# One exp and eight masked copies for eight exps, and the first half of K multiplied in one go, in a decode attention kernel

## Chip, cores, metric

One core of a Trainium2 chip. The metric is the device time of one execution in microseconds (us). All runs quoted are undisturbed ("fast"). The spans in the profiles are 1.7 to 1.9 us shorter than the device times.

## The reference

Attention with one query per head, softmax over all 4096 positions, no mask:

```python
B, H, Sq, Skv, Dh = 8, 32, 1, 4096, 128        # all bf16, normal * 0.05
scores = jnp.einsum('bhqd,bhkd->bhqk', q, k) * Dh ** -0.5
return jnp.einsum('bhqk,bhkd->bhqd', softmax(scores), v)
```

K and V are 268.4 MB each, and each byte is used once.

## The kernel before

The 256 heads go through in 32 tiles of 8 heads. A tile of K or V is 128 partitions x 256 positions x 128 values: 16 partitions per head. K and V tiles take turns in a ring of three buffers. Engines: DVE multiplies K by q in place and folds the products by halves; PE sums what is left over d by multiplying with the identity; DVE reduces these sums to scores and takes the maximum; ACT makes the weights; PE multiplies weights and V.

Three places matter. The multiply of a quarter (UC = MC = 64 positions):

```python
def product(t, lo, hi):
    for c0 in range(lo, hi, MC):
        part = kt[:, c0 : c0 + MC, :]
        nc.vector.tensor_tensor(out=part, in0=part, in1=qb[:].to_broadcast([P, MC, D]), op=ALU.mult)
        nc.vector.tensor_tensor(out=part[:, :, 0 : D // 2], in0=..., in1=..., op=ALU.add)
        ...                          # in quarters 2 and 3 of most tiles a second fold, to D // 4
```

The weights, which must be zero for the 7 heads that do not own a partition:

```python
nc.vector.tensor_scalar(out=bias[:], in0=own[:], scalar1=nmax[:, 0:1], scalar2=None, op0=ALU.add)
for g in range(G):                   # own holds 0 or -1e30 per head: exp gives 0 for a foreign one
    nc.scalar.activation(out=w[:, :, g, :], in_=sc_g, func=ACT.Exp, bias=bias[:, g : g + 1],
                         scale=scale, accum_out=esum[:, t % R, g : g + 1])
```

And the order within a tile, which is fixed by hand for PE, DVE, ACT and the load queue:

```python
product(t, 0, Q);          sum_over_d(t, 0)
...                        # PE: normalisation, result of t-2, q of t+2
product(t, Q, 2 * Q);      sum_over_d(t, 1);  scores_of(t, 0)
product(t, 2 * Q, 3 * Q);  sum_over_d(t, 2);  scores_of(t, 1)
product(t, 3 * Q, C);      sum_over_d(t, 3);  scores_of(t, 2)
if loop:                   # tiles 1 to 29
    values_loop(t - 1)     # 64 matmuls on PE, weights x V of the tile before
    load("k", t + 1); load("v", t)
scores_of(t, 3); weights_of(t)
```

The load of a V tile goes into the buffer of the K tile just used, that of a K tile into the buffer of the V tile that the value loop has just read.

## Time and profile before

| | before |
|---|---|
| time, median of 3 runs | 1252.86 us (1252.73 to 1252.98) |
| load queue, share of 16 DMA engines | 99.4%, mean 430 GB/s |
| DVE / PE / ACT busy | 83% / 62% / 14% |
| one K and V pair | 38.7 us |

### The profile page before, as it was taken

What the parts mean: (1) busy time and instruction counts of PE and PEld (TensorE: products, weight loads), DVE (VectorE), ACT (ScalarE), POOL (GpSimd) and SP (SyncE); (2) the same over time, 40 slices, a digit from 0 to 9 for tenths busy, and PEclk for the clock granted to TensorE, in tenths of its full rate; (3) what the DMA queues carried; (4) which work ended last, traced back from release to release, by engine and by line L of the source; (5) the groups of instructions that cost most, each with busy time, mean ns of one, the idle gap of its engine ahead of it and who ended that gap; (6) DMA issues with size and microseconds to landing.
All of it is one profiled execution on the core that took longest, in us unless ns stands there. A gap on an engine that the chain in (4) does not pass through costs nothing. (4 is left out here: it accounts for less than half of the span.)

```text
span 1250.9 us, 11080 instructions
## 1 busy us (share of the span) xinstructions
PE 770.4 (62%) x3078; PEld 289.4 (23%) x3078; DVE 1036.1 (83%) x586; ACT 170.7 (14%) x625; POOL 3.5 (0%) x19
## 2 busy tenths in 40 slices
PE   3465567755577555775557755577655776557756
PEld 1122122211222212222122221122221222122222
DVE  7887988888978889887798888988889887898783
ACT  0111011111011110111101111011110111101111
POOL 0000000000000000000000000000000000000000
PEclk9977788777887778877778777788777887778867
DMA  9999999999999999999999999999999999999997
GB/s 404 436 436 435 436 436 432 434 436 434 434 424 430 434 434 436 425 434 434 436 436 434 434 434 430 436 428 434 434 430 424 432 437 436 428 428 428 430 445 324
DMA packets 11577, 537.33 MB, mean 430 GB/s; under 512 B 1824, under 2 KB 2080, under 8 KB 2336
## 3 DMA queue, kind: packets, MB, share of 16 engines
q1 hardware_dynamic: 11216, 536.94, 99.4%
q8 instruction: 14, 0.23, 0.1%
q10 hardware_dynamic: 336, 0.07, 0.0%
q14 instruction: 11, 0.09, 0.0%
HBM read 536.94 MB, written 0.07 MB: 429 GB/s over the span
## 5 line engine op out<-in xcount | busy, mean ns | idle before, releaser
L185 DVE TENSOR_TENSOR kt<-kt,qb 128x8192 bf16<-128x8192 bf16 x128 | 565.3, 4416 | 127.9 <-DMA kt<-in_k_dram 103.5
L205 PE MATMUL ps<-kt,ident 128*128 128x512 bf16 x800 | 265.3, 483 | 432.4 <-DVE kt L193 366.8
L289 PE MATMUL av<-vt,w 128*32 x1740 | 426.1, 399 | 3.8
L188 DVE TENSOR_TENSOR kt<-kt 128x4096 bf16<-128x4096 bf16 x128 | 293.4, 2292 | 4.4
L289 PEld LDWEIGHTS av<-vt,w 128*32 x1740 | 174.4, 100 | 261.2 <-issue 114.4
L205 PEld LDWEIGHTS <-ident 128*128 128x128 bf16 x800 | 87.2, 113 | 597.0 <-issue 550.7
L249 ACT ACTIVATE w<-sc,bias 128x256 bf16<-128x256 f32 x256 | 126.3, 494 | 671.6 <-DVE bias L240 671.6
L217 DVE TENSOR_REDUCE sc<-ps 128x64 f32<-128x512 f32 x128 | 87.8, 686 | 57.3 <-PE ps L205 57.3
L193 DVE TENSOR_TENSOR kt<-kt 128x2048 bf16<-128x2048 bf16 x56 | 68.6, 1225 | 1.9
L345 ACT ACTIVATE comb<-av 32x512 bf16<-32x512 f32 (+1 forms) x32 | 18.8, 586 | 321.6 <-PEq L279 313.5
L275 PE MATMUL av<-vt,w 128*32 128x512 bf16 x116 | 47.1, 498 | 14.6 <-issue 13.4
L249 ACT ACTIVATION_READ_ACCUMULATOR w<-sc,bias 128x1 f32 x256 | 47.7, 187 | 0.0
L275 PEld LDWEIGHTS av<-vt,w 128*32 128x32 bf16 x116 | 6.9, 100 | 55.2 <-issue 55.2
L168 ACT ACTIVATE qg<-qh 8x128 bf16<-8x128 f32 x32 | 8.5, 267 | 73.8 <-PE qh L164 73.8
L317 PE MATMUL av<-vt,w 128*32 128x512 bf16 x190 | 14.7, 411 | 1.6 <-DMA vt<-in_v_dram 1.6
L361 PE MATMUL op<-comb,pick 32*16 32x128 bf16 (+1 forms) x128 | 12.3, 215 | 5.1 <-ACT comb L345 5.0
L229 DVE TENSOR_REDUCE pmax<-sc 128x1 f32<-128x256 f32 x32 | 13.4, 420 | 1.1
L170 PE MATMUL qp<-qg,heads 8*128 8x128 bf16 x32 | 6.9, 216 | 11.4 <-ACT qg L168 11.4
L164 PE MATMUL qh<-q_all,ident 128*8 128x128 bf16 x32 | 7.1, 223 | 8.7 <-DMA q_all<-in_q_dram 8.4
L172 ACT ACTIVATE qb<-qp 128x128 bf16<-128x128 f32 x32 | 8.9, 278 | 9.7 <-PE qp L170 9.7
L361 PEld LDWEIGHTS <-pick 32*16 32x16 bf16 (+1 forms) x128 | 6.8, 84 | 12.4 <-issue 12.0
L317 PEld LDWEIGHTS <-w 128*32 128x32 bf16 x190 | 6.5, 103 | 9.9 <-issue 5.5
(29 smaller groups left out, 47.4 us busy)
## 6 DMA issues: line engine op xcount, KB each, us to landing
kt<-in_k_dram SPq DMA_DIRECT2D x6, 4096.0 KB, 24.2
kt<-in_k_dram SPq DMA_DIRECT2D x4, 2048.0 KB, 13.4
vt<-in_v_dram SPq DMA_DIRECT2D x1, 4096.0 KB, 34.6
vt<-in_v_dram SPq DMA_DIRECT2D x1, 2048.0 KB, 39.1
vt<-in_v_dram SPq DMA_DIRECT2D x1, 1024.0 KB, 41.1
vt<-in_v_dram SPq DMA_DIRECT2D x1, 512.0 KB, 41.9
vt<-in_v_dram SPq DMA_DIRECT2D x31, 25.6
kt<-in_k_dram SPq DMA_DIRECT2D x28, 28.1
```

The source lines that it names most:

```text
L185: nc.vector.tensor_tensor(out=part, in0=part, in1=qb[:].to_broadcast([P, MC, D]), op=ALU.mult)
L188: nc.vector.tensor_tensor(out=part[:, :, 0 : D // 2], in0=part[:, :, 0 : D // 2], in1=part[:, :, D // 2 : D], op=ALU.add,)
L193: nc.vector.tensor_tensor(out=part[:, :, 0 : D // 4], in0=part[:, :, 0 : D // 4], in1=part[:, :, D // 4 : D // 2], op=ALU.add,)
L205: nc.tensor.matmul(ps[:], lhsT=ident[:], rhs=kt[:, u * UC : (u + 1) * UC, s * DS : (s + 1) * DS], start=(s == 0), stop=(s == n - 1),)
L217: made = nc.vector.tensor_reduce(out=scs[t][:, u * UC : (u + 1) * UC], in_=sums.pop((t, u))[:], axis=AX.X, op=ALU.add)
L229: nc.vector.tensor_reduce(out=pmax[:], in_=sc[:], axis=AX.X, op=ALU.max)
L249: nc.scalar.activation(out=w[:, :, g, :], in_=sc_g, func=ACT.Exp, bias=bias[:, g : g + 1], scale=scale, accum_out=esum[:, t % R, g : g + 1],)
L275: pe.matmul(av, lhsT=wf[:, i * nw : (i + 1) * nw], rhs=vf[:, i * nv : (i + 1) * nv], **how)
L289: pe.matmul(av, lhsT=wf[:, bass.ds(ow + i * nw, nw)], rhs=vf[:, bass.ds(ov + i * nv, nv)], start=False, stop=False,)
L317: nc.tensor.matmul(avs[t][j * AG : (j + 1) * AG, :], lhsT=w[:, i, :, :], rhs=vt[:, c0 : c0 + CB, :], start=(i < TG), stop=(j not in group[ ...
L345: nc.scalar.activation(out=comb[0:n, :, :], in_=av[0:n, :, :], func=ACT.Copy)
L361: nc.tensor.matmul(ops[n][:], lhsT=pick[0:e, m, r, :], rhs=comb[0:e, m, :], start=(r == 0 and m == 0), stop=(r == R - 1 and m == CB - 1),)
```

## The change

It means to relieve DVE and ACT: ACT computes exp once per tile, sums it once and makes the eight weights by copies scaled with a 0/1 mask; the bias instruction on DVE goes; in the 29 loop tiles the first two quarters of K are multiplied and folded in one instruction each, PE sums both afterwards, and the score reductions of quarters 0 and 1 come behind the third quarter. Core of the diff:

```diff
-    sc_pool = ctx.enter_context(tc.tile_pool(name="sc_pool", bufs=2))
+    sc_pool = ctx.enter_context(tc.tile_pool(name="sc_pool", bufs=1))
...
+    mine = consts.tile([P, R, RG], F32, name="mine")      # 1 where the partition is the head's own
...
-        for c0 in range(lo, hi, MC):
-            part = kt[:, c0 : c0 + MC, :]
+        part = kt[:, lo:hi, :]
...
-        bias = small.tile([P, G], F32, name="bias", tag="bias")
-        nc.vector.tensor_scalar(
-            out=bias[:], in0=own[:], scalar1=nmax[:, 0:1], scalar2=None, op0=ALU.add
+        nc.scalar.activation(
+            out=e[:], in_=sc[:], func=ACT.Exp, bias=nmax[:, 0:1], scale=scale,
+            accum_out=esums[t // R][:, t % R : t % R + 1],
...
-                out=w[:, :, g, :], in_=sc_g, func=ACT.Exp, bias=bias[:, g : g + 1], scale=scale,
-                accum_out=esum[:, t % R, g : g + 1],
+                out=w[:, :, g, :], in_=e_g, func=ACT.Copy, scale=mine[:, 0, g : g + 1]
...
-            product(t, 0, Q)
-            sum_over_d(t, 0)
+            product(t, 0, 2 * Q if loop else Q)
+            if not loop:
+                sum_over_d(t, 0)
...                                                        # results, q of t+2
-            product(t, Q, 2 * Q)
+            if loop:
+                sum_over_d(t, 0)
+            else:
+                product(t, Q, 2 * Q)
             sum_over_d(t, 1)
-            scores_of(t, 0)
+            if not loop:
+                scores_of(t, 0)
             product(t, 2 * Q, 3 * Q)
             sum_over_d(t, 2)
+            if loop:
+                scores_of(t, 0)
             scores_of(t, 1)
```

The normalisation multiplies the sums with the mask in two matmuls instead of with ones in one. The description of the change also names a loop of six value matmuls; that is in both kernels.

More of the change, by code (lines that the diff above doesn't have):

```diff
@@ L46 @@
     NU = C // UC
-    MC = UC
     CB = 4
@@ L118 @@
         )
-    ones = consts.tile([P, 1], F32, name="ones")
-    nc.vector.memset(ones[:], 1.0)
+    mine = consts.tile([P, R, RG], F32, name="mine")
+    nc.gpsimd.memset(mine[:], 1.0)
+    nc.gpsimd.affine_select(
+        out=mine[:], in_=mine[:], pattern=[[PH * G, R], [-PH, RG]], compare_op=ALU.is_ge,
+        fill=0.0, base=0, channel_multiplier=1,
+    )
+    nc.gpsimd.affine_select(
+        out=mine[:], in_=mine[:], pattern=[[-PH * G, R], [PH, RG]], compare_op=ALU.is_ge,
+        fill=0.0, base=PH - 1, channel_multiplier=-1,
+    )
     w_last = consts.tile([P, LAST, RG], BF16, name="w_last")
@@ L182, in product @@
         qb = qbs[t]
-        for c0 in range(lo, hi, MC):
-            part = kt[:, c0 : c0 + MC, :]
+        part = kt[:, lo:hi, :]
+        nc.vector.tensor_tensor(
+            out=part, in0=part, in1=qb[:].to_broadcast([P, hi - lo, D]), op=ALU.mult
+        )
+        nc.vector.tensor_tensor(
+            out=part[:, :, 0 : D // 2], in0=part[:, :, 0 : D // 2],
+            in1=part[:, :, D // 2 : D], op=ALU.add,
+        )
+        if width_of(t, lo // UC) < D // 2:
             nc.vector.tensor_tensor(
-                out=part, in0=part, in1=qb[:].to_broadcast([P, MC, D]), op=ALU.mult
-            )
-            nc.vector.tensor_tensor(
-                out=part[:, :, 0 : D // 2], in0=part[:, :, 0 : D // 2],
-                in1=part[:, :, D // 2 : D], op=ALU.add,
-            )
-            if width_of(t, c0 // UC) < D // 2:
-                nc.vector.tensor_tensor(
-                    out=part[:, :, 0 : D // 4], in0=part[:, :, 0 : D // 4],
-                    in1=part[:, :, D // 4 : D // 2], op=ALU.add,
-                )
+                out=part[:, :, 0 : D // 4], in0=part[:, :, 0 : D // 4],
+                in1=part[:, :, D // 4 : D // 2], op=ALU.add,
+            )
     sums = {}
@@ L238, in weights_of @@
         )
-        bias = small.tile([P, G], F32, name="bias", tag="bias")
-        nc.vector.tensor_scalar(
-            out=bias[:], in0=own[:], scalar1=nmax[:, 0:1], scalar2=None, op0=ALU.add
+        if t % R == 0:
+            esums[t // R] = small.tile([P, R], F32, name="esum", tag="esum")
+        e = o_pool.tile([P, C], BF16, name="e", tag="e")
+        nc.scalar.activation(
+            out=e[:], in_=sc[:], func=ACT.Exp, bias=nmax[:, 0:1], scale=scale,
+            accum_out=esums[t // R][:, t % R : t % R + 1],
         )
         w = w_pool.tile([P, C // CB, G, CB], BF16, name="w", tag="w")
-        if t % R == 0:
-            esums[t // R] = small.tile([P, R, G], F32, name="esum", tag="esum")
-        esum = esums[t // R]
-        sc_g = sc[:].rearrange("p (i m) -> p i m", m=CB)
+        e_g = e[:].rearrange("p (i m) -> p i m", m=CB)
         for g in range(G):
             nc.scalar.activation(
-                out=w[:, :, g, :], in_=sc_g, func=ACT.Exp, bias=bias[:, g : g + 1], scale=scale,
-                accum_out=esum[:, t % R, g : g + 1],
+                out=w[:, :, g, :], in_=e_g, func=ACT.Copy, scale=mine[:, 0, g : g + 1]
             )
@@ L328, in norm_of @@
         zp = ps_z.tile([RG, 1], F32, name="zp", tag="zp")
-        nc.tensor.matmul(
-            zp[:], lhsT=esums.pop(n).rearrange("p r g -> p (r g)"), rhs=ones[:],
-            start=True, stop=True,
-        )
+        esum = esums.pop(n)
+        for r in range(R):
+            nc.tensor.matmul(
+                zp[:], lhsT=mine[:, r, :], rhs=esum[:, r : r + 1], start=(r == 0), stop=(r == R - 1)
+            )
         zps[n] = zp
```

## The prediction

> **What bounds the kernel now.** I read the page's queue part first, because this kernel has to stream all of K and V: 64 tiles of 128x32768 bf16, 8.389 MB each, 536.9 MB in all.
>
> ```profile
> span 1250.9 us, 11080 instructions
> ...
> DMA  9999999999999999999999999999999999999997
> GB/s 404 436 436 435 436 436 432 434 436 434 434 424 430 434 434 436 425 434 434 436 436 434 434 434 430 436 428 434 434 430 424 432 437 436 428 428 428 430 445 324
> ...
> q1 hardware_dynamic: 11216, 536.94, 99.4%
> ```
>
> The load queue takes 99.4% of the time of all 16 engines, and only the first and the last of the 40 slices leave the band of 424 to 445 GB/s. The share of an engine says nothing against this: DVE is busiest at 83%. The chain that ended last says 3% DMA only because it is followed back no further than 1178.38 us; its last long piece is a 41.99 us wait for the last V transfers, which land at 1246.53 us, 4.4 us before the end. So the span is: start of the stream, 64 transfers in a row, and a tail of 4.4 us.
>
> Second, the table of waits, to see whether the engines push the queue or the queue the engines (columns: total us, times, longest):
>
> ```profile
> DVE kt L185 <- DMA kt<-in_k_dram: 103.5, 23, 5.7
> DVE kt L185 <- ACT stage L370: 17.4, 4, 4.4
> ```
>
> DVE waits for K in 23 tiles, 4.5 us each. I take the second line for the same gap under another name: 4 waits of 4.4 us, before a multiply that reads nothing of L370. Thus in 27 tiles DVE is done with over 4 us to spare.
>
> Third, the timeline over one K/V pair, for the moment at which each buffer comes free, because that could starve the queue:
>
> ```profile
> 502.15 0.33 SPq L151 DMA_DIRECT2D vt<-in_v_dram  x1
> ...
> 508.46 4.42 DVE L185 TENSOR_TENSOR kt<-kt,qb 128x8192 bf16<-128x8192 bf16 x1 [4.36 <-DMA kt<-in_k_dram]
> ...
> 519.05 0.33 SPq L151 DMA_DIRECT2D kt<-in_k_dram  x1
> ...
> 540.91 0.33 SPq L151 DMA_DIRECT2D vt<-in_v_dram  x1
> ```
>
> The V load is issued at 502.15, when PE has summed the last quarter of the K tile whose slot it takes. The K transfer ahead of it lands at 508.46. V has therefore stood in the queue 6.3 us before its turn. It lands about 25.6 us after issue (median of the issue table), at 527.8; the next K was issued at 519.05, when the loop of value matmuls had freed the V slot, so 8.7 us early. One pair takes 38.7 us (502.15 to 540.91), and 2 x 8.389 MB / 38.7 us is 434 GB/s, the rate of a full queue. Two stocks matter from here: 6.3 us on V, 8.7 us on K.
>
> [...] the rate over 81.09 to 1091.92 us is 433 GB/s[...]. [...] 4416 ns for 8192 elements and 2292 for 4096 give 0.519 ns per element and 168 ns fixed.
>
> **The change, part by part.** The loop of six is already in the kernel before (LOOP = 6 on both sides, no diff line touches it); it counts as nothing.
>
> Fused halves. In the 29 loop tiles (t = 1 to 29) two multiplies and two adds become one each. Before, the first half of K took 508.46 to 521.79, 13.33 us from start to start. After: multiply 4.42 + 8192 x 0.519 ns = 8.67, add 2.29 + 4096 x 0.519 ns = 4.42, less the 0.08 by which the next start overlaps an add: 13.0. Gain 0.3 us per tile on DVE.
>
> Order of PE. The sums of quarters 0 and 1 (16 matmuls of 0.24 us start to start, 3.8 us) now begin together at about 508.46 + 13.1 = 521.6, where quarter 0 began at 519.07. Before them PE now does the little normalisation, combining and q matmuls; the value loop ends at 518.9, the copy of its result on ACT ends at 519.7, the small matmuls need some 1.3 us more with their two ACT steps: 521.0, just ahead of DVE. The sums end at 525.4. DVE meanwhile does the third quarter (4.45 + 2.33 + 1.15 = 7.9 us from 521.5 to 529.4), so both score reductions find their sums ready; they take 1.3 us together. Fourth quarter: 530.7 to 538.6, 0.15 us less if no reciprocal falls in. Last PE sum from 538.7, V issue near 540.6 where it was 540.91. The V stock grows by 0.3 us instead of shrinking.
>
> Softmax. Per tile, DVE loses the bias instruction (0.23 us). ACT did eight exps of 0.49 us start to start (504.13 to 508.18, 4.05 us), each with an accumulator read of 0.19. Now: one exp and read, 0.6 us, about 0.1 for the wait on its own result, then eight copies of 256 elements with a pointer scale[...], together 3.9 to 4.0 us. ACT is a wash, and its results are needed only at the next value loop, over 30 us later. ACT waits 671.6 us in total for L240, so it bounds nothing.
>
> Normalisation sum: matmuls on the mask instead of the ones; 32 become 64 at 0.17 us, 5.4 us more PE time over 16 places, all in the gap after the value loop. The mask costs GpSimd three instructions of about 0.2 us near 4 us; the first copy needs it past 42 us.
>
> One score buffer. The next tile's first score reduction waits for the exp of this tile. That exp ends near 504.8, the reduction now starts near 529.4. No wait, by 24 us.
>
> Queue. The order of loads and their sizes are the same. Two semaphore waits move in the last tiles: one on the first half of K 29 goes from the V load to the last piece of K 31, and that half landed long before. Tail and first K tile are untouched, except for one 0.23 us bias that ends with the weights at 1238.2, while PE still waits for V at 1242.24 and 1246.57.
>
> Sum: DVE saves 29 x 0.3 + 32 x 0.23 = 16 us, all of it given back as a longer wait for K (from about 4.4 to about 4.9 us per tile). On the end: 0. The stream is as long as before. I take 1252.7, the median within its own noise (1252.73 to 1252.98).
>
> **Rivals.** (a) DVE is the true bound: then 16 us come off and the time is 1237. For it: 83% busy, by far the largest share. Against: it waits for K in 27 tiles, and the queue is at 99.4%. (b) The later and bunched PE sums delay the V load. They would have to eat 6.3 us, less the start of a transfer (the first load is issued at 0.74 us and the engines are 51% busy in the first 2 us, so under 1 us); a delay of 8 us, a whole quarter on DVE, would cost 8 - 5.3 = 2.7 us x 29 = 78 us and give 1331. Against: the walk above has V leaving 0.3 us earlier. (c) PE meets the loop at a lower clock: the granted clock falls to 0.50 in the stretches without matmuls (526 to 544 us) and the longer gap after the loop might let it stay there. The matmuls at half clock run at 0.43 us start to start, so a whole loop of 64 would take 27 us instead of 16.7, and the K stock of 8.7 us would be gone: 10.6 - 8.7 = 2 us per tile, 3 with the start of a transfer, so 1310 to 1340. Against: the gap that grows lies behind the loop (519 to 521.6), is short, and holds small matmuls; the first loop, at 75.84 to 92.1, began just as cold. (d) The single buffers chain ACT to DVE: spoken for only by the extra waits, refuted by 24 us of distance.
>
> **Range and chances.** Repeats spread by 0.25 us, and single tiles by about 1 us (pairs of 40.05 and 39.65 us among those of 38.6), with loads issued early all the same, so this jitter is the stream's own. Over some 26 pairs it sums to about 7 us; a different draw may move the time by 1 or 2 us. Range 1250.0 to 1255.5. Faster by over 2% would need 1227.8, below 536.94 MB at 436 GB/s (1231.5) even without start and tail: 0.5%. Slower by over 2% needs (b) or (c) in full: 1.5%.
>
> **What would show it.** Right: queue share again 99% and 430 GB/s mean; multiply of 128x16384 at 8.6 to 8.7 us x29; [...] DVE busy near 1020 us; its waits for K longer, about 4.9 us; V issued 6 us or more, K 8 us or more before the transfer ahead lands. Wrong: slices under 420 GB/s in the middle, a queue share under 98%, or a loop that ends after the V ahead has landed.

With them the sum for ACT came to 3.9 to 4.0 us per tile; the terms of the eight copies are cut, what stands of the terms is 0.6 us for the exp with its read and about 0.1 for the wait. (The changed kernel's trace has 0.60 us, from 504.13 to 504.73; 0.12 from the end of the exp to the first copy; and 3.30 for the eight copies.) That overlap cannot raise the rate, and that the mix of DVE and ACT accesses does not move it, was not shown at that point. No run here shows that 436 GB/s is a limit; it is the rate in many slices of the trace. For DVE's accesses, experiment 1 measures the rate. The granted clock that rival (c) speaks of is, in the trace before, 1.00 over 524 to 526 us, 0.79 over 526 to 528 and 0.50 over 528 to 544; PE has no matmul from 524 to 530.4 us.

## The result

| | before | changed |
|---|---|---|
| median, 6 runs each | 1252.86 us (1252.73 to 1252.99) | 1252.43 us (1251.73 to 1253.19) |
| DVE busy | 1036.1 us | 1021.9 us |
| ACT busy | 170.7 us | 166.0 us |
| PE busy | 770.4 us | 775.5 us |

The ratio is 0.9996, 95% interval 0.9984 to 1.0009: the same time. (A ratio here is the mean time of one kernel's fast runs over that of the other's of the same rounds, so not quite the ratio of the medians.)

From the page of the changed kernel, the queue:

```profile
GB/s 405 436 436 434 434 436 434 436 434 428 430 428 434 435 430 432 436 434 434 436 436 432 428 436 430 436 434 434 426 432 436 434 433 430 428 426 436 427 446 322
...
q1 hardware_dynamic: 11216, 536.94, 99.4%
```

The rate, the share and the two slow ends are those of before. From its groups by shape (busy us, mean ns, idle before):

```profile
L192 DVE TENSOR_TENSOR kt<-kt,qb 128x16384 bf16<-128x16384 bf16 x29 | 252.0, 8690 | 135.0 <-DMA kt<-in_k_dram 135.0
L195 DVE TENSOR_TENSOR kt<-kt 128x8192 bf16<-128x8192 bf16 x29 | 128.3, 4425 | 1.0
L256 ACT ACTIVATE w<-e,mine 128x256 bf16<-128x256 bf16 x256 | 105.6, 495 | 1.1
```

One wide multiply takes 8.69 us where two took 8.83; a copy takes as long as an exp did (495 against 494 ns). And its table of waits:

```profile
DVE kt L192 <- DMA kt<-in_k_dram: 135.7, 28, 6.3
```

27 of these waits are those of loop tiles 2 to 28, 135.0 us or 5.0 us each; before, the same tiles waited 120.9 us (the two lines of the prediction), 4.5 us each. The 14.2 us of DVE work saved came back as 14.1 us more of waiting for K. The timeline of the same pair of tiles as in the prediction:

```profile
502.36 0.33 SPq L159 DMA_DIRECT2D vt<-in_v_dram  x1
...
504.76 3.30 ACT L256 ACTIVATE w<-e,mine 128x256 bf16<-128x256 bf16 x8
508.92 8.69 DVE L192 TENSOR_TENSOR kt<-kt,qb 128x16384 bf16<-128x16384 bf16 x1 [4.89 <-DMA kt<-in_k_dram]
...
519.20 0.33 SPq L159 DMA_DIRECT2D kt<-in_k_dram  x1
...
522.12 5.30 PE L212 MATMUL ps<-kt,ident 128*128 128x512 bf16 x16 [1.19 <-DVE kt L195]
...
541.11 0.33 SPq L159 DMA_DIRECT2D vt<-in_v_dram  x1
```

V is issued 6.6 us before the K ahead of it lands (6.3 before), and the pair takes 38.75 us.

One line had not been expected. K of tile 29 is loaded in two halves, so DVE can start on it without a wait for K, 1.5 us after the value loop at the end of tile 28 has begun. The kernel before, tile 29, on DVE (start us, us, instruction, idle before and its releaser):

```profile
1126.21 4.43 DVE L185 TENSOR_TENSOR kt<-kt,qb 128x8192 bf16<-128x8192 bf16 x1
...
1143.28 0.69 DVE L217 TENSOR_REDUCE sc<-ps 128x64 f32<-128x512 f32 x1 [3.65 <-PE ps L205]
```

The changed kernel:

```profile
1125.21 8.66 DVE L192 TENSOR_TENSOR kt<-kt,qb 128x16384 bf16<-128x16384 bf16 x1
...
1145.83 0.69 DVE L224 TENSOR_REDUCE sc<-ps 128x64 f32<-128x512 f32 x1 [0.24 <-PE ps L212]
```

Before, DVE stood 3.65 us until PE was through with the loop and had summed quarter 0; with the later score reductions the wait is 0.24 us. The next V load leaves at 1156.89 us where it left at 1161.59, and the last tile's weights are ready some 6 us earlier (its value matmuls then wait 2.98 us for V at 1236.86). The end does not move: the last V lands at 1246.1 where it landed at 1246.5.

So in the one tile where DVE does not wait for K while a value loop still runs (in tile 1 none runs yet), the change is worth 3.7 us: from the tile's first multiply to the next V load 35.4 us before, 31.7 after. That gave the theory to test: **the stream of loads is the bound and hides the change; but the reserve behind it was small before and is large after, and that comes from the order of the score reductions.** The rivals: DVE is the bound, or the two parts of the change offset each other.

### The profile page after: what moved, and what is told of

It reads as the page before. It is cut to its first block, busy times and chain, and to the rows that moved or that the text cites. A ratio compares the mean times of both kernels' runs of the same rounds, so it can differ in the third digit from the quotient of the medians.

```text
span 1250.4 us, 10830 instructions
## 1 busy us (share of the span) xinstructions
PE 775.5 (62%) x3110; PEld 296.6 (24%) x3110; DVE 1021.9 (82%) x495; ACT 166.0 (13%) x433; POOL 4.0 (0%) x22
## 3 DMA queue, kind: packets, MB, share of 16 engines
q1 hardware_dynamic: 11216, 536.94, 99.4%
## 5 line engine op out<-in xcount | busy, mean ns | idle before, releaser
L192 DVE TENSOR_TENSOR kt<-kt,qb 128x8192 bf16<-128x8192 bf16 (+1 forms) x99 | 560.9, 5665 | 142.6 <-DMA kt<-in_k_dram 135.7
L195 DVE TENSOR_TENSOR kt<-kt 128x4096 bf16<-128x4096 bf16 (+1 forms) x99 | 288.8, 2917 | 3.4
L212 PEld LDWEIGHTS <-ident 128*128 128x128 bf16 x800 | 92.4, 116 | 564.4 <-issue 519.5
L224 DVE TENSOR_REDUCE sc<-ps 128x64 f32<-128x512 f32 x128 | 85.4, 685 | 53.1 <-PE ps L212 53.1
L249 ACT ACTIVATE e<-sc,nmax 128x256 bf16<-128x256 f32 x32 | 16.3, 508 | 702.0 <-DVE nmax L243 702.0
L256 ACT ACTIVATE w<-e,mine 128x256 bf16<-128x256 bf16 x256 | 105.6, 495 | 1.1
L200 DVE TENSOR_TENSOR kt<-kt 128x2048 bf16<-128x2048 bf16 x56 | 68.6, 1225 | 1.9
```

The source lines that it names most:

```text
L195: nc.vector.tensor_tensor(out=part[:, :, 0 : D // 2], in0=part[:, :, 0 : D // 2], in1=part[:, :, D // 2 : D], op=ALU.add,)
L200: nc.vector.tensor_tensor(out=part[:, :, 0 : D // 4], in0=part[:, :, 0 : D // 4], in1=part[:, :, D // 4 : D // 2], op=ALU.add,)
L212: nc.tensor.matmul(ps[:], lhsT=ident[:], rhs=kt[:, u * UC : (u + 1) * UC, s * DS : (s + 1) * DS], start=(s == 0), stop=(s == n - 1),)
L224: made = nc.vector.tensor_reduce(out=scs[t][:, u * UC : (u + 1) * UC], in_=sums.pop((t, u))[:], axis=AX.X, op=ALU.add)
L249: nc.scalar.activation(out=e[:], in_=sc[:], func=ACT.Exp, bias=nmax[:, 0:1], scale=scale, accum_out=esums[t // R][:, t % R : t % R + 1],)
L256: nc.scalar.activation(out=w[:, :, g, :], in_=e_g, func=ACT.Copy, scale=mine[:, 0, g : g + 1])
```

## The experiments

### 1. The parts alone, and hardly any DVE work

Two kernels carry one part of the change each. The third is the kernel before with an eighth of the multiply and no adds (a wrong result):

```diff
-            part = kt[:, c0 : c0 + MC, :]
+            part = kt[:, c0 : c0 + MC // 8, :]
...
-            nc.vector.tensor_tensor(out=part[:, :, 0 : D // 2], ...)    # and the second fold
```

> The kernel before with the softmax part alone (one exp, eight masked copies, mask in the normalisation, one score buffer). Theory (the load queue is the bound): same time, 1252 to 1253.5 us; DVE busy about 7 us less than 1036, ACT busy 4 to 5 us less than 171, DVE's wait for K about 0.2 us longer per tile. Rival (DVE is the bound): 7 us less, 1245. Rival (two parts of the change offset each other): over 5 us away from 1252.9 in either direction.

> The kernel before with the fused halves and the later score reductions alone, softmax as before. Theory (the load queue is the bound): same time, 1251.5 to 1253.5 us; the 3.65 us wait of DVE for PE in tile 29 is gone and the last tiles run some 4 us earlier, given back as a wait for V. Rival (DVE is the bound): 9 us less, 1244. Rival (the parts offset each other): over 5 us away from 1252.9, on the side opposite to the softmax part.

> The kernel before with the multiply on an eighth of the columns and no adds: wrong results on purpose, DVE work cut from some 32 to some 6 us per tile, loads unchanged. Theory (the load queue is the bound, and DVE's accesses do not slow it): 1249 to 1253 us, queue share over 99%. Rival (DVE is the bound, or the chain through DVE and PE): well under 1230 us. Rival (DVE's accesses slow the transfers): the mean rate rises above 432 GB/s and the time falls by 5 us or more.

The kernel before took 1252.73 us on this chip (9 runs).

| run | median us | ratio to before (95%) | DVE busy us |
|---|---|---|---|
| softmax_only | 1252.98 (5 runs) | 1.0002 (0.9988 to 1.0016) | 1028.3 |
| order_only | 1253.84 (5 runs) | 1.0007 (0.9993 to 1.0020) | 1029.3 |
| light_dve | 1252.90 (4 runs) | 0.9999 (0.9983 to 1.0014) | 202.4 |

Neither part moves the time clear of noise (the median of order_only lies 0.3 us over the guess; the interval of its ratio holds 1, although each of its five runs lies above the nine of before, by 0.1 to 1.6 us), so no two effects of more than about 1 us offset each other. In order_only, too, the 3.65 us wait of tile 29 is gone. The third run is the sharpest. From its table of waits:

```profile
DVE kt L185 <- DMA kt<-in_k_dram: 837.4, 35, 28.9
```

834 us of DVE work are gone, DVE's wait for K rises from 121 to 837 us and its wait for PE from 57 to 163 us, and the time stands; the queue's share is 99.4% again. The mean rate in the middle (80 to 1120 us) is 433 GB/s, as before: DVE's accesses do not slow the transfers here. DVE is not the bound.

### 2. How large was the reserve?

Two idle DVE reductions (measured 1.21 us each) ahead of the last quarter in each loop tile, in four kernels:

```diff
+            if loop:
+                for _ in range(2):
+                    nc.vector.tensor_reduce(out=idle[:], in_=<128x1024 view of ident>, axis=AX.X, op=ALU.max)
             product(t, 3 * Q, C)
```

> The kernel before with two idle DVE reductions (about 1.2 us each, estimated) ahead of the last quarter's multiply in each of the 29 loop tiles. New theory: the true reserve of the kernel before is not the 4.4 us that DVE waits for K but about 0.9 us. As soon as DVE starts a K tile less than 3.5 us behind the end of its predecessor, the value loop on PE still runs when DVE wants the sums of quarter 0, and DVE waits for PE, up to 3.5 us as in tile 29. Pair time then 34.3 + 2.4 + 3.5 = 40.2 us in place of 38.7: 1295 us (1280 to 1310). Rival, the reading of the prediction: reserve 4.4 us, so 1252 to 1254 us.

> The changed kernel with the same two idle reductions. Theory: the later score reductions take the wait for PE away, the reserve is the whole 4.9 us wait for K (or 3.7 of it), so 1252 to 1254 us. Rival (reserve no larger than that of before): 1280 us or more.

> The softmax part alone with the two idle reductions. Theory: it gives DVE only the 0.23 us of the bias, so 34.06 + 2.4 + 3.5 = 40.0 us per pair: about 7 us less than the delayed kernel before, 1288 us (1273 to 1303). Rival (the softmax part carries the reserve): 1252 to 1254 us.

> The fused halves and later score reductions alone with the two idle reductions. Theory: this part carries the reserve, 1252 to 1254 us. Rival (the softmax part carries it): 1280 us or more.

The kernel before took 1252.79 us on this chip.

| run | median us (4 runs) | ratio to before (95%) |
|---|---|---|
| delay2_before | 1298.26 | 1.0362 (1.0345 to 1.0379) |
| delay2_softmax | 1297.09 | 1.0353 (1.0335 to 1.0370) |
| delay2_after | 1261.27 (1258.33 to 1266.90) | 1.0078 (1.0048 to 1.0109) |
| delay2_order | 1263.20 (1262.01 to 1266.95) | 1.0088 (1.0068 to 1.0107) |

In the kernel before, 2.4 us of DVE work per tile cost 45 us, 1.57 us per loop tile, although DVE waited 4.4 us for K in nearly every tile. Its timeline shows the cause: no wait for K any more, a wait for PE instead.

```profile
376.87 0.33 SPq L153 DMA_DIRECT2D kt<-in_k_dram  x1
376.90 1.89 PE L207 MATMUL ps<-kt,ident 128*128 128x512 bf16 x8 [0.19 <-PEq L281]
...
378.89 0.69 DVE L219 TENSOR_REDUCE sc<-ps 128x64 f32<-128x512 f32 x1 [3.54 <-PE ps L207]
...
388.09 2.44 DVE L418 TENSOR_REDUCE idle<-ident 128x8 f32<-128x1024 bf16 x2
...
419.54 0.69 DVE L219 TENSOR_REDUCE sc<-ps 128x64 f32<-128x512 f32 x1 [3.84 <-PE ps L207]
```

The 2.44 us instruction pair is the addition; the brackets on the score reductions are DVE waiting until PE has left the value loop (PEq) and done 8 sums. It works out from the undisturbed trace. There the loop ends 10.4 us after K lands (508.46 to 518.9), and DVE wants quarter 0 summed 13.3 us after. The loop starts when DVE has finished the tile before; so each microsecond by which DVE's wait for K shrinks moves the loop's end a microsecond nearer to, then past, that moment. With no wait for K left, the loop ends 14.8 us after the start, the sums come 1.9 later, and DVE waits some 3.5 us. DVE's wait for PE eats more of the wait for K, which makes the wait for PE longer: past the edge it runs up to its full size. The edge is at 4.4 - 3.5 = 0.9 us, and the run agrees: 2.44 us of work cost 1.57 us, so 0.87 us were free.

The order part moves the edge past 2.4 us: in delay2_order DVE waits 53.1 us in all for PE, against 143.5 us in delay2_before. The softmax part does not move it: I had expected about 7 us less than delay2_before and got 1.2 us less. Its 8.0 us less of DVE work (1097.5 against 1105.5 us busy) came back as 7.8 us more of waiting for PE (151.3 against 143.5 us). In the timeline above the bias instruction runs beside the value loop and not in the ring that sets the pace there: value loop, sums of quarter 0, score reduction, the later quarters, value loop. The fused halves and the later reductions were not run apart; that the later reductions carry the order part is read from the timeline, not shown.

But the two kernels with the order part did not stay at 1253, as I had expected. Something took 8 to 10 us, and DVE still waited for K in them (delay2_after):

```profile
DVE kt L194 <- DMA kt<-in_k_dram: 78.0, 27, 4.9
```

### 3. Where do these 8 us come from?

The same two reductions at the end of the tile, behind the softmax statistics. There they fill DVE's wait for K and move neither the V load nor the value loop:

```diff
             weights_of(t)
+            if loop:
+                ...                                  # the same two reductions
```

> The kernel before with the two idle DVE reductions (1.21 us each, measured) at the end of each loop tile, behind the softmax statistics, in place of ahead of the last quarter. There they move neither the V load, nor the start of the value loop, nor PE; they only fill DVE's wait for K. Theory: 1252 to 1254 us, DVE's wait for K about 2.0 us in place of 4.4, no wait for PE at quarter 0. Rival (any 2.4 us of DVE work costs the kernel before what it cost in delay2_before): 1290 us or more.

> The changed kernel with the same two reductions at the end of the tile. It tells where the 6 to 10 us of delay2_after come from. Theory: from the V load, issued 2.4 us later there and so only some 4 us ahead of its turn; here it keeps its 6.5 us, so 1252 to 1254 us. Rival (from DVE's shorter wait for K itself): 1258 to 1266 us as in delay2_after.

| run | median us (4 runs) | ratio to before (95%) | wait for K, us each |
|---|---|---|---|
| delay2end_before | 1254.18 | 1.0013 (0.9996 to 1.0030) | 2.1 |
| delay2end_after | 1253.77 | 1.0006 (0.9990 to 1.0023) | 2.6 |

The waits are from these lines, delay2end_before first (it has three more waits, 5.8 us together, under names of ACT):

```profile
DVE kt L187 <- DMA kt<-in_k_dram: 51.3, 24, 3.2
```

```profile
DVE kt L194 <- DMA kt<-in_k_dram: 71.3, 27, 4.0
```

Both stand within noise of the kernel before (1252.73 us), the first a little over the guess. So the wait for K is free at the end of the tile, and the same work ahead of the last quarter is not: 1254 against 1298 us in the kernel before, 1254 against 1261 in the changed one. In the second pair the difference is the moment of the loads. From delay2_after:

```profile
702.11 0.33 SPq L161 DMA_DIRECT2D vt<-in_v_dram  x1
...
706.25 8.69 DVE L194 TENSOR_TENSOR kt<-kt,qb 128x16384 bf16<-128x16384 bf16 x1 [2.46 <-DMA kt<-in_k_dram]
```

V left at 702.11 us and the K ahead landed at 706.25, 4.1 us later, where the changed kernel has 6.6; K loads leave 2.4 us later too. Pairs of 40 or 41 us (for instance 940.88 to 981.93) become more frequent among those of 38.7. Shown is that the work costs 8 us at this place and none at the other. That it does so through the later issue is argued: DVE still waits for K, so the stream still sets the pace, and only the issues reach it. The queue's share is still 99.3%, but its rate falls from 433 to 429 GB/s in the middle of the span.

The kept trace holds more than its views print: each load lands in 16 parts, taken here as one per DMA engine, and each packet has its own time. In these two kernels the parts of one K load land spread over 1.2 to 4.3 us. In the changed kernel the first part lands 3.9 us (median) after the V load behind it was issued; in delay2_after 2.4 us, once only 0.63. Between 80 and 1120 us delay2_after moves 3.8 MB less than the changed kernel, worth some 9 us. In that stretch an engine stands idle about 3 us longer, all told and on average, and its packets of 64 KB take about 6.6 us longer, nearly all of it in the 10 us behind the V issues. So engines that finish early do run dry, and the lead that counts seems to be that before the first part. Why the packets get slower stays open.

### 4. With fewer bytes, and beyond the reserve

V tiles 0 to 28 are loaded in their first half only, and the value matmuls, as many as before, read parts of that half again (wrong; shown in part):

```diff
     cuts = {
+        **{("v", t): [C // 2] for t in range(NT - 3)},
...
-                pe.reg_add(rv, rv, LOOP * nv)
+                pe.reg_add(rv, rv, 0)
```

The last run puts six idle reductions into the changed kernel ahead of the last quarter. The kernel before took 1252.74 us on this chip.

> The kernel before with V tiles 0 to 28 loaded only in their first half, which the value matmuls read again (wrong results on purpose): 122 MB less. If the load queue is the bound of before, the time falls until the next bound; theory: that is the DVE work of 34.3 us and its 3.5 us wait for PE, 37.8 us per pair, hardly under the 38.7 of the loads: 1225 to 1240 us. Rival (reserve 4.4 us): 34.3 to 35.5 us per pair, 1130 to 1165 us.

> The changed kernel with the same halved V. Theory: no wait for PE; DVE work of 33.7 us, but K is issued only at the end of the value loop and lands some 35 us after the K before, so 33.7 to 35.5 us per pair: 1115 to 1165 us, 70 to 110 us under the halved kernel before. Rival (the change gives only 0.5 us per tile): 15 us under it.

> The changed kernel with six idle reductions (about 7.2 us). Theory: beyond the reserve of 4.9 us; pair time 33.7 + 7.2 = 40.9 us, with up to 1.2 us more of wait for PE: 1315 to 1350 us. Rival (DVE work is hidden altogether): 1253 us.

| run | median us (4 runs) | ratio to before (95%) |
|---|---|---|
| halfv_before | 1213.92 | 0.9689 (0.9672 to 0.9705) |
| halfv_after | 1152.47 | 0.9198 (0.9182 to 0.9213) |
| delay6_after | 1325.14 | 1.0577 (1.0560 to 1.0595) |

With 23% fewer bytes the kernel before gains 3%, the changed one 8%; between them lie 61 us. Both guesses were off by some 10 us (1225 to 1240, and 70 to 110 us of difference), the direction holds. The waits of DVE in the halved kernel before (total us, times, longest):

```profile
DVE sc L218 <- PE ps L206: 136.4, 61, 3.2
...
DVE kt L186 <- DMA kt<-in_k_dram: 2.3, 4, 0.9
```

And in the halved changed kernel:

```profile
DVE sc L225 <- PE ps L213: 52.5, 33, 3.1
DVE kt L193 <- DMA kt<-in_k_dram: 42.0, 21, 4.4
```

In the first, DVE hardly waits for K, and for PE 84 us more than in the second: 37.5 us per tile (451.36 to 488.88), only 1.2 under the 38.7 of the full loads. In the second the wait for PE is down to that of the undisturbed kernels (57.3 before, 53.1 changed), and K is late again: it can be issued only when the loop has freed a buffer. The load stream of the original kernels thus hid a second bound lying 3% below it, and the change moved that second bound away. delay6_after falls into its range: 7.3 us of added work (1.22 each) are beyond the reserve of 4.9, (1325.14 - 1252.74) / 29 = 2.5 us per loop tile too much, and DVE has stopped waiting for K.

PE is not the bound either: halfv_after does as many matmuls and is 100 us faster than the changed kernel. No version that loads all bytes beats both kernels: none of them makes the stream shorter.

## Why the prediction was right, point by point

- **The bound.** The load queue, read from 99.4% and the waits for K. Confirmed by light_dve: a fifth of the DVE work (202.4 against 1036.1 us busy), the same time (1252.90 us).
- **Fused halves.** Predicted 8.67 us for the wide multiply and 4.42 for the add; measured 8.69 and 4.43.
- **ACT a wash.** Predicted 3.9 to 4.0 us per tile; measured from 504.13 to 508.06 us, 3.93. Copies 495 ns, eight in 3.30 us.
- **Sum.** Predicted 16 us less on DVE, given back as a wait of 4.9 us; measured 14.2 us less busy and 5.0 us (from 4.5).
- **Time.** 1252.7 predicted, 1252.43 measured. V leaves 6.6 us and K some 9 us ahead, as said.
- **Two terms that were off without harm.** The 16 sums of quarters 0 and 1 were put at 3.8 us and took 5.30 (522.12 to 527.42): the prediction took their pace right behind the loop, but now PE first waits 1.19 us for DVE, and the clock granted to PE is 0.50 of full speed over 524 to 526 us, where they start 0.43 us apart (0.24 behind the loop in the kernel before). DVE asks for them only at 529.9. The normalisation matmuls were put at 5.4 us more of PE time and took 0.6 (3.2 to 3.8). The loop itself was not slowed, which rival (c) allowed for: 16.2 us against 16.3.
- **The step that was wrong without harm.** "Thus in 27 tiles DVE is done with over 4 us to spare." The wait is real, the spare time was not: work of 2.4 us at the end of a tile cost nothing (1254), ahead of the last quarter 45 us (1298). The reserve there, worked out and measured above, was 0.9 us. The forecast of the time does not rest on this step, since the change takes work from DVE and adds none. I looked at each wait by itself and did not ask what else moves when DVE gets later: the value loop on PE, and with it the next tile's sums.
- **Rival (b)** counted the stock on V as free down to some 1 us, so that a delay under 5.3 us would cost nothing. The work that made the issue 2.4 us later already cost 8 us (delay2_after against delay2end_after). The start of a transfer was also put too low: the first packets move at 1.76 us, 1.0 us after the first issue at 0.74, and the 16 parts of the load ahead end up to 4.3 us apart.
- **Tile 29** was overlooked: it is a loop tile in which DVE does not wait for K, and it ran 3.7 us faster. The stream hid that too.

## What to carry to other kernels

When one transfer stream fills its queue (99.4% here), ask of a change first whether loads leave later: here V loads issued some 4.1 us ahead of the end of the K load, in place of 6.6, went with a loss of 8 us over the run. Work saved elsewhere came back as waiting: 14.2 us less of DVE work, 14.1 us more of waiting for K. An engine's idle time was a reserve only at the place where it lay: the same 2.4 us per tile cost nothing clear of noise at the end of the tile (1254 us) and 45 us ahead of the last quarter (1298). So before calling it spare, follow what starts later when that engine is late, through the other engines and back. A change that gains nothing may still widen the distance to the next bound: with V halved the two kernels lay 61 us apart. Delay the suspected engine by a known amount, at two places, to measure that distance.
